# A scheduler that may let VectorE or GpSimd stand still for the port they share, with all its ranks set anew

## The chip, the cores and the metric

One core of a Trainium2 chip. The metric is the device time of one execution in microseconds (us), lower is better. The core has TensorE (matrix multiply, PE in the profile, its weight loads PEld), VectorE (DVE), ScalarE (ACT), GpSimd (POOL) and SyncE (SP), which here issues the DMAs. Each engine runs its own instructions strictly in the order in which the program gives them.

## The reference

```python
# q, k, v: (2, 8, 576, 64); three stages, all float32
scores = q @ k.T / sqrt(64)
kth = np.partition(scores, -32, axis=-1)[..., -32:-31]
attn = softmax(np.where(scores >= kth, scores, -1e9))
x = (attn @ v)                       # -> (1152 tokens, 512)
h = x @ moe_w_in;  x = (h * np.tanh(log1p(exp(h)))) @ moe_w_out    # 512 -> 2048 -> 512
h = x @ moe2_w_in; out = (h * sigmoid(h)) @ moe2_w_out             # 512 -> 2048 -> 512
```

The weights arrive as 64-bit floats and are turned into 32-bit floats on the chip.

## The kernel before

**Tiles.** The 1152 tokens are nine tiles of 128. Attention works on a tile and a pair of heads: 36 such pairs, four to a tile. A pair's way is: the q tile is split into a high and a low part (`qs`, line 279 or 277 for the high part, 285 or 287 for the low one), TensorE makes the scores (L373, `ps_att`), ScalarE or VectorE copies them to `sc`, VectorE finds the 32 largest of each row by four MAX8 (L389, `m`) and three MATCH_REPLACE8 (L392, `rest`) a head. Then, for tiles 0 to 5, ScalarE makes the exponentials `e` (L405) and VectorE masks and sums them (L409, which reads `sc` and `e`); for tiles 6 to 8 a mask is made by ScalarE (L415), subtracted on GpSimd or VectorE (`e` on L285 or L287) and ScalarE's exponential sums (L422). TensorE turns `e` (L434), the copies go to `pt`, TensorE multiplies by `v` (L450, L452, `ps_misc`), the row sums are inverted, spread and turned (L457 to L466), and VectorE multiplies (L475) into `xt`, the input of the first block. Line numbers of helpers stand for many uses: L277 is a copy on ScalarE, L279 one on VectorE, L285 a two-input operation on GpSimd, L287 the same on VectorE.

**Blocks.** The two feed-forward blocks take the tiles in groups: block 1 in [0], [1], [2], [3,4], [5,6], [7,8]; block 2 in [0,1], [2], [3,4], [5,6], [7,8]. Groups marked 'n' multiply in plain float32, groups marked 'r' with operands split into two parts and three passes. A group's first product is L625 (`ps_h`; L717 for the very first group), its second L696 (block 1) or L803 (block 2) into `ps_y`. Group [0,1] of block 2 needs block 1 of both tiles. 64 weight units are converted the first time they are used (L500 twice and L512 on ScalarE, L504 and L514 on GpSimd, the last giving `wraw`) and stored as float32 in DRAM; the 'r' groups split them again into `ws` (L277/L279, L285/L287), or read the splits back.

**Order.** `Plan` writes the whole program's order. `add` notes a step with the ways to do it (an engine, a cost, a flex added to the rank, and whether it takes the port that VectorE and GpSimd share: all of GpSimd's, and VectorE's fast copies and two-input operations from SBUF). A step's rank is its tile's or group's start plus a step (`TILES`, `DUE1`, `DUE2`), less the boost of its kind (`OFF`), plus the flex of its way (`FLEX`, or `FLEX1` for ranks below `EARLY`). `emit` then plays the program with its own costs: of all the steps that could go next it takes the one with the least key, a time first and the rank second. A step that can begin within `PEEK` of its engine's free time has that free time as its key, so steps of one engine are then sorted by rank. `port` is the time at which the shared port comes free. No step computes anything else for being placed elsewhere; only the order on each engine, the engine of steps with two ways, and the order of the DMA issues depend on these numbers.

Of the kernel before, what the change touches and what calls it, by code (L numbers as in the profile page):

```python
# [28 lines left out]
BLOCK1 = [([0], 'n'), ([1], 'n'), ([2], 'n'), ([3, 4], 'r'), ([5, 6], 'r'), ([7, 8], 'r')]  # L29
BLOCK2 = [([0, 1], 'n'), ([2], 'n'), ([3, 4], 'r'), ([5, 6], 'r'), ([7, 8], 'r')]  # L30

TILES = [(27.37, 9.86), (57.91, 10.94), (103.1, 10.19), (209.13, 7.03), (210.76, 10.65), (248.61, 48.9), (293.47,
         17.23), (429.14, 22.89), (434.19, 29.14)]
DUE1 = [(59.64, 30.74), (73.56, 12.7), (180.72, 34.18), (251.34, 30.85), (303.68, 119.16), (534.81, 11.0)]
DUE2 = [(192.15, 71.0), (274.42, 49.15), (480.58, 43.53), (598.12, 89.99), (800.13, 295.82)]

SBUF_BUFS = dict(kraw=1, kk=5, v=5, qraw=2, qs=2, sc=4, rest=1, e=1, pt=2, m8=10, bias=10, den=8, x=3, dt=2, xt=1,
                 wraw=9, ws=8, hs=2, th=1, wide=3, y=2, o=2)
PSUM_BUFS = dict(att=2, misc=1, h=3, y=2)

FLEX = dict(khi=-194.73, klo=-148.49, qhi=-16.01, qlo=-130.13, whi=-223.66, wlo=264.55, ghi=-13.66, glo=-274.69,
            hs=253.61, mk=197.2, se=96.17, den=6.96, y=300.0, sc=-176.69, pt=185.3, dt=-250.49, xlo=300.0)
FLEX1 = dict(khi=77.4, klo=230.65, qhi=-36.04, qlo=246.7, whi=-229.64, wlo=-300.0, ghi=-164.53, glo=194.85, hs=254.09,
             mk=120.49, se=None, den=-73.24, y=None, sc=300.0, pt=None, dt=267.41, xlo=-300.0)
EARLY = 566.61

OFF = dict(kload=416.67, qload=339.58, k=13.66, q=-14.61, sp=196.22, sc=127.3, bias=145.14, e=187.12, tp=155.23,
           pt=377.16, av=14.57, x=469.8, den=223.26, dw=224.3, dp=142.13, xt=253.71, m=0.66, cload=-5.6, cpn=-65.41,
           cse=12.49, cw=-42.16, cmid=46.37, wload=312.03, wsplit=-142.7, wstore=141.3, g=-146.58, hs=-58.75, y=394.7,
           th=516.12)  # L50

PEEK = 0.1
ADD = 1

HBM = 4
# [13 lines left out]
class Plan:  # L69
# [12 lines left out]
    def add(self, ways, reads=(), writes=(), uses=(), rank=0.0, boost=0.0, table=None, load=0.0):  # L82
# [3 lines left out]

        first = rank - (boost if not isinstance(boost, str) else OFF[boost])
        offset = lambda o: o if not isinstance(o, str) else FLEX1[o] if rank < EARLY and o in FLEX1 else FLEX[o]
        ways = [(w[0], w[1], offset(w[2]), w[3], w[4] if len(w) > 4 else w[0] == "pool") for w in ways
# [16 lines left out]
    def emit(self):  # L106
        steps = self.steps
        last, readers, users, turn = {}, {}, {}, {}
        for i, s in enumerate(steps):
            deps = set()  # L110
            for k in s["reads"]:
                deps |= last.get(k, set())
            for k in s["writes"]:
                deps |= last.get(k, set()) | readers.get(k, set())
            deps.discard(i)
            s["deps"], s["then"] = len(deps), []
            s["at"] = 0.0
            for d in deps:
                steps[d]["then"].append(i)
            for k in s["writes"]:  # L120
                last[k], readers[k] = {i}, set()
            for k in s["reads"]:
                readers.setdefault(k, set()).add(i)
            for k, t in s["uses"]:
                if k not in users:
                    turn.setdefault(t, []).append((s["rank"], len(users), k))
                users[k] = users.get(k, 0) + 1
        turn = {t: [k for _, _, k in sorted(v, reverse=True)] for t, v in turn.items()}
        free = {e: 0.0 for e in ("pe", "dve", "act", "pool", "sp")}
        dma, hw, port = 0.0, 0.4, 0.0  # L130
        table = None
        slots = {t: [0.0] * n for t, n in self.bufs.items()}
        held, ends, bank = set(), {}, {}
        queue, waiting = {e: set() for e in free}, {}
        for i, s in enumerate(steps):
            if not s["deps"]:
                for w in s["ways"]:
                    queue[w[0]].add(i)
        left = len(steps)
        while left:  # L140
            best = None
            stuck = []
            for e, q in queue.items():
                for i in q:
                    s = steps[i]
                    way = next(w for w in s["ways"] if w[0] == e)
                    at = max(s["at"], free[e], port if way[4] else 0.0)
                    took = {}
                    for k, t in s["uses"]:
                        if k not in held:  # L150
                            n = took[t] = took.get(t, 0) + 1
                            if len(slots[t]) < n or turn[t][-n] != k:
                                at = None
                                stuck.append((t, i))
                                break
                            at = max(at, slots[t][n - 1])
                        elif k in bank and bank[k][0] != e:
                            at = max(at, bank[k][1])
                    if at is None:
                        continue  # L160
                    rank = s["first"] + way[2]
                    key = (at, rank, i) if at > free[e] + PEEK else (free[e], rank, i)
                    if best is None or key < best[0]:
                        best = (key, e, i, at)
            if best is None:
                raise RuntimeError("no step can start")
            for t, i in stuck:
                for w in steps[i]["ways"]:
                    queue[w[0]].discard(i)
                waiting.setdefault(t, set()).add(i)  # L170
            _, e, i, at = best
            s = steps[i]
            moved = set()
            for w in s["ways"]:
                queue[w[0]].discard(i)
            _, cost, _, fn, shared = next(w for w in s["ways"] if w[0] == e)
            for k, t in s["uses"]:
                if k not in held:
                    held.add(k)
                    slots[t].pop(0)  # L180
                    turn[t].pop()
                    moved.add(t)
                    ends[k] = 0.0
            if s["table"] and s["table"] != table:
                cost += self.TABLE
                table = s["table"]
            at = max(at, free[e])
            if e == "pe":
                end = self.run_pe(at, cost)
            else:  # L190
                end = at + cost
            fn()
            free[e] = end
            if shared:
                port = end
            if e == "sp":
                hw = max(hw, at) + 0.55
                dma = max(dma, hw + 1.0) + s["load"] / 335e3
                end = max(end, dma + 1.4 - self.WAIT["sp"])
            for k, t in s["uses"]:  # L200
                if t.startswith("ps_"):
                    bank[k] = (e, end + self.WAIT[e])
                ends[k] = max(ends[k], end)
                users[k] -= 1
                if not users[k]:
                    slots[t].append(ends[k] + self.WAIT[e])
                    slots[t].sort()
                    moved.add(t)
            for t in moved:
                for j in waiting.pop(t, ()):  # L210
                    for w in steps[j]["ways"]:
                        queue[w[0]].add(j)
            for j in s["then"]:
                n = steps[j]
                n["at"] = max(n["at"], end + self.WAIT[e])
                n["deps"] -= 1
                if not n["deps"]:
                    for w in n["ways"]:
                        queue[w[0]].add(j)
            left -= 1  # L220
# [19 lines left out]
def kernel(ctx: ExitStack, tc, qh, kh, va, w1i, w1o, w2i, w2o, out):  # L240
# [580 lines left out]
    ystep = {}  # L821
    for t, (start, step) in enumerate(TILES):
        for p in range(NPAIR):
            attention(t, p, start + p * step)
    for g, (start, us) in enumerate(DUE1):
        block1(g, start, us)
    for g, (start, us) in enumerate(DUE2):
        block2(g, start, us)
# [48 lines left out]
```

## Time and profile before

| | |
|---|---|
| median of 3 runs | 670.81 us (668.43 to 670.87) |
| profiled execution | 671.01 us, span 669.2 us |
| busy | PE 606.7, PEld 534.9, DVE 533.7, ACT 468.0, POOL 392.2 us |
| moved by DMA | 178.32 MB |

The span is the time from the first to the last instruction in the profile; the profiled execution's own time is 1.8 us above it. A busy time is the sum of an engine's instructions, overlaps counted once. Groups of the profile list what ended the idle time before an instruction ("<-").

### The profile page before, as it was taken

To read this page: it belongs to the slowest core of one execution; us is meant where nothing else is said; L and a number is where in the kernel's file an instruction comes from. 1 tells how busy PE (TensorE), PEld (TensorE's weight loads), DVE (VectorE), ACT (ScalarE), POOL (GpSimd) and SP (SyncE) were. 2 spreads that over 40 slices of the span, in tenths; PEclk is the share of its full clock that TensorE was granted. 3 is DMA by queue.
4 is the path that set the end of the run, shared out by engine and by line. 5 is a ranking of instruction groups with operands and counts; after the bars stand their busy time and mean duration, and the time that the engine had idled before them with its cause. 6 is when DMAs were issued, how large, how long until landed. Compare 5 with 4: busy or idle time off the path is not lost.

```text
span 669.2 us, 13044 instructions
## 1 busy us (share of the span) xinstructions
PE 606.7 (91%) x4536; PEld 534.9 (80%) x4536; DVE 533.7 (80%) x1111; ACT 468.0 (70%) x973; POOL 392.2 (59%) x347
## 2 busy tenths in 40 slices
PE   1359857999999999989999999999999999999997
PEld 1248746998999966668799858999988799999996
DVE  4999998998999999799989898999989332434451
ACT  6779898699599999979985644977884543322321
POOL 6987648636477779886674212748973224554440
PEclk9999876999999999999999999999999999999999
DMA  9958538888899777899799797884669989876752
GB/s 311 314 175 256 193 120 282 281 289 302 272 299 323 243 227 274 272 349 317 266 369 409 226 325 238 279 272 155 219 228 305 369 289 320 285 244 236 268 174 82
DMA packets 85649, 178.32 MB, mean 266 GB/s; under 512 B 8144, under 2 KB 29136, under 8 KB 85584
## 3 DMA queue, kind: packets, MB, share of 16 engines
q1 hardware_dynamic: 85584, 177.50, 78.6%
q8 instruction: 35, 0.57, 0.3%
q14 instruction: 30, 0.25, 0.1%
HBM read 138.94 MB, written 38.54 MB: 265 GB/s over the span
## 4 chain that ended last, share of the span: by engine, by line
PE 46%; DVE 26%; ACT 15%; DMA 5%; issue 5%; POOL 2%; SPq 0%; DVEq 0%; ACTq 0%; POOLq 0%
PE ps_h L625 19%; DVE m L389 10%; PE ps_y L803 9%; PE ps_y L696 9%; DVE rest L392 8%; ACT ws L500 3%; PE ps_att L373 3%; PE ps_misc L450 3%; DVE e L409 2%; PE ps_att L434 2%; DMA wide<-in_w1i_dram 2%; DVE ws L287 2%; ACT wraw L512 2%; ACT pt L277 2%; ACT sc L277 1%
## 5 line engine op out<-in xcount | busy, mean ns | idle before, releaser
L389 DVE MAX8 m<-rest 128x8 f32<-128x576 f32 x216 | 155.4, 751 | 0.1
L285 POOL TENSOR_TENSOR ws<-wraw,ws 128x512 fp32r<-128x512 f32 x57 | 74.1, 1306 | 60.2 <-DVE ws L279 50.6
L504 POOL TENSOR_TENSOR ws<-ws 128x512 int32<-128x512 int32 x64 | 86.5, 1357 | 36.4 <-ACT ws L500 33.8
L392 DVE MATCH_REPLACE8 rest<-m,rest 128x576 f32<-128x576 f32 x144 | 106.8, 746 | 0.0
L500 ACT ACTIVATE ws<-wide,zone 128x512 int32<-128x512 int16 x128 | 94.8, 773 | 6.2 <-DMA wide<-in_w1o_dram 4.0
L373 PE MATMUL ps_att<-kk,qs 128*128 128x288 f32 x320 | 70.6, 341 | 26.9 <-POOL kk L285 17.1
L514 POOL TENSOR_TENSOR wraw<-wraw,ws 128x512 int32<-128x512 int32 x64 | 84.3, 1326 | 14.3 <-ACT wraw L512 10.7
L373 PEld LDWEIGHTS ps_att<-kk,qs 128*128 128x128 f32 x320 | 50.2, 202 | 35.5 <-POOL kk L285 24.8
L625 PEld LDWEIGHTS ps_h<-y,ws 128*128 128x128 f32 x576 | 73.3, 188 | 2.9
L625 PE MATMUL ps_h<-y,ws 128*128 128x256 f32 x576 | 75.6, 280 | 0.0
L625 PE MATMUL ps_h<-xt,ws 128*128 128x256 f32 x576 | 72.4, 282 | 0.1
L696 PE MATMUL ps_y<-wide,ws 128*128 128x256 f32 x540 | 71.2, 283 | 0.0
L625 PEld LDWEIGHTS ps_h<-xt,ws 128*128 128x128 f32 x576 | 69.3, 188 | 1.6 <-issue 1.0
L434 PE MATMUL ps_att<-ident,e 128*128 128x128 f32 x324 | 53.4, 289 | 17.7 <-DVE e L409 12.0
L696 PEld LDWEIGHTS ps_y<-wide,ws 128*128 128x128 f32 x540 | 66.2, 188 | 0.0
L803 PE MATMUL ps_y<-ws,wide 128*128 128x512 f32 x252 | 64.6, 396 | 0.0
L285 POOL TENSOR_TENSOR wide<-hs,wide 128x512 fp32r<-128x512 f32 x24 | 35.2, 1473 | 46.0 <-DVE wide L279 39.7
L434 PEld LDWEIGHTS ps_att<-ident,e 128*128 128x128 f32 x324 | 38.6, 147 | 28.4 <-DVE e L409 14.7
L696 PE MATMUL ps_y<-hs,wraw 128*128 128x128 f32 x384 | 52.3, 283 | 8.1 <-POOL wraw L514 4.5
L277 ACT COPY sc<-ps_att 128x288 f32<-128x288 f32 x120 | 44.9, 404 | 16.8 <-PE ps_att L373 16.2
L696 PEld LDWEIGHTS ps_y<-hs,wraw 128*128 128x128 f32 x384 | 48.6, 197 | 9.5 <-POOL wraw L514 5.4
L389 DVE MAX8 m<-sc 128x8 f32<-128x576 f32 x72 | 53.0, 751 | 2.1 <-ACT sc L277 1.8
(88 smaller groups left out, 1222.0 us busy)
## 6 DMA issues: line engine op xcount, KB each, us to landing
wraw<-w1i SPq DMA_DIRECT2D x64, 256.0 KB, 5.0
wraw<-w2i SPq DMA_DIRECT2D x64, 256.0 KB, 3.7
ws<-w1o_split SPq DMA_DIRECT2D x30, 512.0 KB, 4.8
ws<-w2o_split SPq DMA_DIRECT2D x28, 512.0 KB, 3.9
wraw<-w1o SPq DMA_DIRECT2D x48, 256.0 KB, 5.2
wide<-in_w1i_dram SPq DMA_DIRECT2D x16, 512.0 KB, 5.9
wide<-in_w1o_dram SPq DMA_DIRECT2D x16, 512.0 KB, 4.4
wide<-in_w2i_dram SPq DMA_DIRECT2D x16, 512.0 KB, 4.7
```

What stands on the lines that cost most here:

```text
L277: ways.append(("act", act_us(n, psum), act, lambda: nc.scalar.copy(get_out(), get_in())))
L285: ways.append(("pool", pool_us(n), pool, lambda: nc.gpsimd.tensor_tensor(out=get_out(), in0=get_a(), in1=get_b(), op=op)))
L373: nc.tensor.matmul(o, lhsT=l, rhs=r[:, f * SH:(f + 1) * SH], start=(i == 0), stop=(i == len(ops) - 1))
L389: add([("dve", 0.67, 0, lambda i=i, h=h, src=src: nc.vector.max(out=m8()[:, h, 8 * i:8 * i + 8], in_=src()[:, h]))], reads=srck, writes=[K ...
L392: add([("dve", 0.73, 0, lambda i=i, h=h, src=src: nc.vector.match_replace(out=rest()[:, h], in_to_replace=m8()[:, h, 8 * i:8 * i + 8], in_ ...
L434: nc.tensor.transpose(o[:, i, :], ef[:, (c + i) * P:(c + i + 1) * P], ident)
L500: add([("act", act_us(UNIT) + 0.14, 0, lambda i=i: nc.scalar.activation(pn()[:, i], top(), AF.Relu, scale=ONE16 - 2 * ONE16 * i, bias=zone))],
L504: ways = [("pool", pool_us(UNIT), 0, lambda: nc.gpsimd.tensor_tensor(out=se(), in0=pn()[:, 0], in1=pn()[:, 1], op=ALU.subtract))]
L514: add([("pool", pool_us(UNIT), 0, lambda: nc.gpsimd.tensor_tensor(out=w().bitcast(I32), in0=w().bitcast(I32), in1=se(), op=ALU.add))], rea ...
L625: nc.tensor.matmul(hp[:, c, :], lhsT=l, rhs=rr, start=(i == 0), stop=(i == len(ops) - 1))
L696: nc.tensor.matmul(yp[:, o, :], lhsT=l[:, d * P:(d + 1) * P], rhs=rr[:, c, :], start=(fc == 0 and k == 0 and o == 0), stop=last, skip_grou ...
L803: nc.tensor.matmul(op, lhsT=gg[:, c, i * P:(i + 1) * P], rhs=wt, start=(fc == 0 and k == 0), stop=(fc == NFC - 1 and k == len(ops) - 1))
```

## The change

The scheduler's loop used to put the port into a step's earliest time: a step that needs the port later than `PEEK` after its engine's free time was sorted by the time at which the port comes free, behind any step that can begin at once. Now the port is looked at apart: a step that waits for the port alone, and for at most `PORT` = 0.34 us, is still sorted by rank at its engine's free time, so the engine may stand still for it. `PEEK` falls from 0.1 to 0.05. All ranks, boosts and flexes have new values.

```diff
-TILES = [(27.37, 9.86), (57.91, 10.94), (103.1, 10.19), (209.13, 7.03), (210.76, 10.65), (248.61, 48.9), (293.47,
-         17.23), (429.14, 22.89), (434.19, 29.14)]
-DUE1 = [(59.64, 30.74), (73.56, 12.7), (180.72, 34.18), (251.34, 30.85), (303.68, 119.16), (534.81, 11.0)]
-DUE2 = [(192.15, 71.0), (274.42, 49.15), (480.58, 43.53), (598.12, 89.99), (800.13, 295.82)]
+TILES = [(19.37, 6.76), (46.36, 14.1), (106.73, 4.63), (204.37, 9.99), (225.06, 11.69), (258.55, 49.85), (345.98,
+         18.22), (519.3, 17.23), (461.45, 16.83)]
+DUE1 = [(55.53, 32.57), (72.6, 11.18), (185.18, 33.6), (264.74, 3.6), (326.98, 167.36), (749.26, 11.24)]
+DUE2 = [(194.98, 61.15), (262.2, 26.21), (504.62, 78.52), (783.18, 203.62), (946.46, 197.95)]
...
-FLEX = dict(khi=-194.73, klo=-148.49, qhi=-16.01, qlo=-130.13, whi=-223.66, wlo=264.55, ghi=-13.66, glo=-274.69,
-            hs=253.61, mk=197.2, se=96.17, den=6.96, y=300.0, sc=-176.69, pt=185.3, dt=-250.49, xlo=300.0)
-FLEX1 = dict(khi=77.4, klo=230.65, qhi=-36.04, qlo=246.7, whi=-229.64, wlo=-300.0, ghi=-164.53, glo=194.85, hs=254.09,
-             mk=120.49, se=None, den=-73.24, y=None, sc=300.0, pt=None, dt=267.41, xlo=-300.0)
-EARLY = 566.61
+FLEX = dict(khi=-199.43, klo=-179.86, qhi=-300.0, qlo=65.82, whi=259.95, wlo=-153.31, ghi=-62.92, glo=163.54,
+            hs=286.73, mk=-58.0, se=-300.0, den=105.07, y=271.68, sc=-47.47, pt=57.06, dt=-238.16, xlo=98.83)
+FLEX1 = dict(khi=245.84, klo=30.36, qhi=-26.57, qlo=179.72, whi=-172.94, wlo=-208.13, ghi=-191.1, glo=300.0, hs=19.48,
+             mk=8.23, se=None, den=-282.09, y=None, sc=252.9, pt=None, dt=239.76, xlo=-232.84)
+EARLY = 553.02
...
-OFF = dict(kload=416.67, qload=339.58, k=13.66, q=-14.61, sp=196.22, sc=127.3, bias=145.14, e=187.12, tp=155.23,
-           pt=377.16, av=14.57, x=469.8, den=223.26, dw=224.3, dp=142.13, xt=253.71, m=0.66, cload=-5.6, cpn=-65.41,
-           cse=12.49, cw=-42.16, cmid=46.37, wload=312.03, wsplit=-142.7, wstore=141.3, g=-146.58, hs=-58.75, y=394.7,
-           th=516.12)
-
-PEEK = 0.1
+OFF = dict(kload=578.07, qload=135.46, k=16.71, q=-13.88, sp=314.62, sc=197.87, bias=39.06, e=246.77, tp=342.92,
+           pt=330.03, av=-14.23, x=487.41, den=300.22, dw=35.2, dp=222.21, xt=191.17, m=-75.12, cload=96.71,
+           cpn=-97.42, cse=5.37, cw=-99.8, cmid=-37.21, wload=572.6, wsplit=-171.63, wstore=206.7, g=-82.77, hs=-40.2,
+           y=-31.25, th=709.1)
+
+PEEK = 0.05
+
+PORT = 0.34
...
-                    at = max(s["at"], free[e], port if way[4] else 0.0)
+                    at = max(s["at"], free[e])
...
-                    key = (at, rank, i) if at > free[e] + PEEK else (free[e], rank, i)
+                    soon = at <= free[e] + PEEK
+                    if way[4] and port > at:
+                        at, soon = port, soon and port <= free[e] + PORT
+                    key = (free[e] if soon else at, rank, i)
```

## Rows read from the trace of the kernel before

**Rows 1.** The page's head, busy times, slices and the chain by engine.
```profile
span 669.2 us, 13044 instructions
PE 606.7 (91%) x4536; PEld 534.9 (80%) x4536; DVE 533.7 (80%) x1111; ACT 468.0 (70%) x973; POOL 392.2 (59%) x347
...
PE   1359857999999999989999999999999999999997
...
DVE  4999998998999999799989898999989332434451
...
PE 46%; DVE 26%; ACT 15%; DMA 5%; issue 5%; POOL 2%; SPq 0%; DVEq 0%; ACTq 0%; POOLq 0%
```

**Rows 2.** Busy time by stretch: PE, PEld, DVE, ACT, POOL, then clock and DMA.
```profile
0.00:53.00 53.00, 19.66 (x97) 15.55 (x98) 41.93 (x88) 40.05 (x78) 43.03 (x44) 1.00 0.83 261
53.00:121.00 68.00, 54.23 (x398) 46.02 (x397) 63.91 (x142) 62.21 (x133) 43.43 (x37) 0.85 0.64 211
121.00:205.00 84.00, 83.06 (x704) 79.08 (x703) 80.28 (x177) 69.33 (x137) 46.95 (x49) 1.00 0.88 299
205.00:345.00 140.00, 134.33 (x969) 107.83 (x968) 135.43 (x284) 130.88 (x277) 110.10 (x97) 1.00 0.84 286
345.00:425.00 80.00, 77.02 (x602) 65.68 (x601) 70.32 (x153) 45.54 (x108) 27.61 (x28) 1.00 0.87 302
425.00:530.00 105.00, 102.94 (x816) 94.27 (x815) 92.56 (x195) 77.36 (x180) 67.26 (x55) 1.00 0.76 259
530.00:669.20 139.20, 135.47 (x963) 126.46 (x961) 49.27 (x78) 42.69 (x66) 53.87 (x41) 1.00 0.71 241
```

**Rows 3.** Groups of VectorE from 9 to 121 us: busy us, mean ns, idle before.
```profile
L389 DVE MAX8 m<-rest 128x8 f32<-128x576 f32 x50 | 36.0, 752 | 0.1
...
L409 DVE SCALAR_TENSOR_TENSOR e<-sc,m,e 128x576 f32<-128x576 f32 x16 | 16.2, 1044 | 0.5 <-ACT e L405 0.5
...
L279 DVE COPY sc<-ps_att 128x288 f32<-128x288 f32 x8 | 3.6, 456 | 9.2 <-PE ps_att L373 9.0
```

**Rows 4.** VectorE in order of time, 6 to 12, 39 to 50 and 112 to 122 us.
```profile
8.70 0.94 DVE L279 COPY sc<-ps_att 128x288 f32<-128x288 f32 x2 [8.70 <-PE ps_att L373]
...
40.53 1.97 DVE L409 SCALAR_TENSOR_TENSOR e<-sc,m,e 128x576 f32<-128x576 f32 x1
...
113.13 0.29 DVE L475 TENSOR_TENSOR xt<-ps_misc,dt 128x128 f32<-128x128 f32 x1 [1.56 <-PE ps_misc L452]
...
114.70 0.82 DVE L409 SCALAR_TENSOR_TENSOR e<-sc,m,e 128x576 f32<-128x576 f32 x1
...
120.40 0.28 DVE L475 TENSOR_TENSOR xt<-ps_misc,dt 128x128 f32<-128x128 f32 x1
```

**Rows 5.** GpSimd in order of time, 39 to 50 us.
```profile
39.95 1.93 POOL L285 TENSOR_TENSOR kk<-kraw,kk 64x576 fp32r<-64x576 f32 x1
```

**Rows 6.** Lines L409 and L287, the whole span: ns min/median/max, first and last start.
```profile
L409 DVE SCALAR_TENSOR_TENSOR e<-sc,m,e x48: 795/818/1967, 39.8 to 398.3; 128x576 f32<-128x576 f32 x48
...
L287 DVE TENSOR_TENSOR ws<-wraw,ws x52: 672/690/1791, 280.8 to 556.4; 128x512 fp32r<-128x512 f32 x52
```

**Rows 7.** Groups of the whole span, shapes apart.
```profile
L504 POOL TENSOR_TENSOR ws<-ws 128x512 int32<-128x512 int32 x64 | 86.5, 1357 | 36.4 <-ACT ws L500 33.8 <-DMA wraw<-w1o 1.0 <-DMA wraw<-w1i 0.8
L514 POOL TENSOR_TENSOR wraw<-wraw,ws 128x512 int32<-128x512 int32 x64 | 84.3, 1326 | 14.3 <-ACT wraw L512 10.7 <-issue 1.2 <-POOL qs L285 1.1
...
L409 DVE SCALAR_TENSOR_TENSOR e<-sc,m,e 128x576 f32<-128x576 f32 x48 | 44.5, 959 | 0.6 <-ACT e L405 0.5
...
L287 DVE TENSOR_TENSOR ws<-wraw,ws 128x512 fp32r<-128x512 f32 x52 | 43.2, 860 | 5.3 <-ACT ws L277 5.0
...
L625 PE MATMUL ps_h<-y,ws 128*128 128x256 f32 x576 | 75.6, 280 | 0.0
...
L803 PE MATMUL ps_y<-ws,wide 128*128 128x512 f32 x252 | 64.6, 396 | 0.0
...
L285 POOL TENSOR_TENSOR e<-sc,e 128x576 f32<-128x576 f32 x24 | 34.3, 1448 | 12.2 <-ACT e L415 12.2
```

**Rows 8.** Waits of TensorE: 53 to 121 us, then 205 to 345 us.
```profile
PE ps_y L696 <- POOL wraw L514: 4.5, 2, 2.6
PE ps_y L696 <- issue: 3.4, 1, 3.4
...
PE ps_h L625 <- POOL wraw L514: 2.7, 2, 1.4
PE ps_att L373 <- ACT sc L277: 1.3, 2, 1.1
```

**Rows 9.** Line L514, the whole span: first and last start.
```profile
L514 POOL TENSOR_TENSOR wraw<-wraw,ws x64: 1266/1280/1875, 12.2 to 323.7; 128x512 int32<-128x512 int32 x64
```

**Rows 10.** The chain that ended last, its end: start us, us, what.
```profile
530.47 18.37 PE ps_h L625 x156
...
655.66 9.82 PE ps_y L803 x42
```

**Rows 11.** VectorE in order of time, 515 to 531 us: the last attention pair.
```profile
529.18 0.29 DVE L475 TENSOR_TENSOR x<-ps_misc,dt 128x128 f32<-128x128 f32 x1 [2.24 <-PE ps_misc L452]
```

**Rows 12.** Groups from 205 to 345 us: conversions on GpSimd.
```profile
L514 POOL TENSOR_TENSOR wraw<-wraw,ws 128x512 int32<-128x512 int32 x28 | 37.5, 1348 | 4.5 <-ACT wraw L512 2.4 <-issue 1.2 <-POOL qs L285 0.2
```

## The prediction

> **What bounds the kernel now.** I read the page first: TensorE is busy for 606.7 of 669.2 us, its slices are thin only at the start, and the chain that ended last is 46% TensorE and 26% VectorE [rows 1]. So the question is where TensorE's other 62.5 us lie. The table of stretches answers it (stretch less busy time): 33.3 us from 0 to 53, 13.8 from 53 to 121, 0.9 to 205, 5.7 to 345, 3.0 to 425, 2.1 to 530, 3.7 to the end [rows 2]. Three quarters lie before 121 us. There VectorE is the bound: from its first instruction at 8.7 us it is busy for 41.9 + 63.9 = 105.8 of 112.3 us [rows 2, 4], mostly on the top-32 search [rows 3] of tiles 0 and 1. What ends the stretch can be named: the last product of tile 1 starts at 120.40 us [rows 4]; only then has TensorE the first block of tile 1 and, behind it, the second block of group [0,1].
>
> From 205 to 345 us nothing is slack: VectorE 135.4, ScalarE 130.9, TensorE 134.3 of 140 us [rows 2], with the rest of the weight conversions in it (the last L514 starts at 323.7 [rows 9]). From 530 us on TensorE runs without a break: 156 matmuls in 18.37 us, 118 ns each, at the end 42 in 9.82, 234 ns each [rows 10]. Nothing an order can do makes this stretch shorter, unless work leaves it for a hole further ahead.
>
> A busy matmul row hides its own slack: the weight loads are busy 79.1 of 84 us from 121 to 205, but 107.8 of 140 from 205 to 345 [rows 2]. Part of that is other matmul shapes, so I take the 5.7 us as a lower bound of what that stretch has to give.
>
> **How much VectorE may be delayed later.** The last pair's product is made at 529.2 us [rows 11]; 140 us of span follow. What must come after it is group [7,8] in both blocks: 576 L625 matmuls belong to three groups, 192 each, at 118 ns 22.6 us; block 1's second product is of the same count and shape; block 2's is (252 + 36 on kept weights) / 3 = 96 at 234 ns, 22.5 us [rows 7, 10]. Together some 90 us. So attention may end up to about 50 us later without setting the end, provided that TensorE has other groups to work on meanwhile. VectorE's own time counts up to 121 us and hardly behind it.
>
> **The change, part by part.** No arithmetic is added or removed; engines of steps with two ways, order, and DMA order move.
>
> *The port rule.* What it can act on is the time that port users lose. L409 takes 818 ns in the median and up to 1967 [rows 6]; the 1.97 us one at 40.53 us lies beside a GpSimd operation of 1.93 us from 39.95 to 41.88 [rows 4, 5]. Over the span, L409 loses 48 x (959 - 818) = 6.8 us and the low parts on L287 52 x (860 - 690) = 8.8 us [rows 6, 7]; up to 121 us, 16 x (1044 - 818) = 3.6 us [rows 3, 6]. The rule does not forbid these losses; it lets an urgent port user go ahead of a MAX8 when the port is at most 0.34 us away, and pays with an idle engine. Bounds up to 121 us: a gain of the 3.6 us at the most; a loss of 17 port users (16 L409 and a cast) x 0.34 = 5.8 us if each waits its full third. A MAX8 put in between holds VectorE for 0.75 us [rows 3], longer than the wait it fills, and behind an L409 stand the turn, the copy, the values and the product (114.70 to 120.40 for tile 1's last [rows 4]), so I take 1 us of gain. PEEK's halving goes with it at nothing: the work it shifts is at most 0.1 us apart.
>
> The trace's long stalls are around 1 us, not a third: 1.97 - 0.82 = 1.15 us for the one at 40.53 [rows 4, 6]. The Trainium skill (SBUF — State Buffer, Who interferes with whom) says why that is the natural size: whoever issues first holds the shared pair for its whole instruction and the other is blocked, whatever a plan meant. By that rule each stand-still that the plan sets at 0.34 us could become a whole GpSimd operation, 1.3 us; by the row the plan's wait and the chip's agree in most cases, since most L409 take the median. The trace bears the rule out at 40.53. I give it a rival of its own below.
>
> *Tiles and the first 121 us.* Tiles 0, 1 and 2 keep their order on VectorE: search ranks 19 to 40, 46 to 89, 107 to 121 now, against 27 to 57, 58 to 91, 103 to 134. MAX8 and MATCH_REPLACE8 have no boost, so the same pairs follow one another. What can move is the idle 112.3 - 105.8 = 6.5 us [rows 2] and the score copies on VectorE, 3.6 us [rows 3]. The scores' boost rises by 118, the score copies' by 71, the turns' by 188: the next pair's scores should be there sooner, and gaps like the 1.56 us before 113.13 us [rows 4], in which VectorE waited for TensorE, are those that this fills. Against it, VectorE's flex for score copies falls by 47, which can put more of them there. Bounds 0 to 6.5 us of gain; I take 3, the smaller half, since some gaps are latency of a single pair. With the port's 1 us, tile 1 is ready 4 us sooner and TensorE's full stretch begins 4 us sooner.
>
> *Conversions.* Boosts fall by 32 (cpn, ScalarE), 84 (cmid, ScalarE), 58 (cw, GpSimd) and 7 (cse), and the loads rise by 102. A unit is two L500 and one L512 on ScalarE, and L504 and L514, 1.36 + 1.33 us, on GpSimd [rows 7]. TensorE waited for L514 4.5 us up to 121 us and 2.7 us from 205 to 345 [rows 8]. Before 121 such a wait costs what it delays in attention behind it in TensorE's order, otherwise nothing, as TensorE lacks work anyway. Behind 205 it costs its whole length. GpSimd was busy 110 of 140 us there [rows 2], so conversions ranked later can still find room; ScalarE, at 131, has little. Bounds: +5.7 us of gain if all waits go; for the loss see the rivals.
>
> *Low parts, masks, copies.* The mask's flex falls from 120 to 8, so some of 24 L285 `e` go to VectorE. Each there costs about 690 x 576/512 = 780 ns (an estimate from L287 [rows 6]); all 24, 18.6 us, within the 50 us of allowance, and VectorE's idle time from 205 to 530 us (4.6 + 9.7 + 12.4 = 26.7 us [rows 2]) takes part of it: nothing on the end. The keys' low part, GpSimd's so far (1.93 us in [rows 5]), can now be VectorE's (its flex falls from 231 to 30); that shortens the way to the scores of a new pair and costs VectorE as much as one mask: nothing either. The `y` copies lose 426 of boost; there are groups enough to cover a late copy up to 530 us, and behind it the other open group covers it. DUE1[3] becomes a burst (30.9 to 3.6 us), and the last two block 2 groups now overlap (783 to 987, 946 to 1144), which gives TensorE a second stream where it is full already: nothing.
>
> *Sum.* 4 us up to 121, and 2.5 from 205 to 345 (just under half of 5.7, as the stretch is crowded on every engine), nothing elsewhere: 6.5. The span becomes 662.7; with the 1.8 us around it, 664.5 against 671.0 of the profiled execution, which stands 0.2 above the median of 670.8. Predicted: 664.5 us, its own range 655 to 667.5.
>
> **Rivals.** Half a per cent (667.5 to 674.2 us) is about what a measurement here can tell from no change.
>
> *Nothing moves.* The order of the searches stays, TensorE's full stretches stay full, and the 6.5 us of idle are latency. For it: the same first tiles; the full tail. Against it: 10 us of waits in the first 121 that a better order could cover. 667.5 to 674; chance 0.22.
>
> *Conversions come late (slower).* From 205 us on, L514 with its lower rank stands behind low parts on GpSimd and TensorE, in strict order, waits for `wraw`. 28 L514 fall in the stretch [rows 12]; each one late by one GpSimd operation costs 1.33 us [rows 7] on a full TensorE. Five of them cancel the gain of 6.5 (6.7 us); ten leave 671.0 - 6.5 + 13.3 = 677.8, fourteen 683. For it: 2.7 us of such waits already [rows 8], ScalarE at 94%. Against it: GpSimd's spare 30 us. 675 to 685; chance 0.21.
>
> *The stand-still becomes a full stall (slower).* 17 port users up to 121 us; if six more of them meet a whole GpSimd operation (1.15 us as at 40.53), that is 6.9 us on the stretch where VectorE sets the end, and with the other gains lost 671.0 + 6.9 = 677.9. It decides from about three on, 3.5 us. The page named above is the reason to expect it. Against it: half of the 48 L409 take 818 ns or less [rows 6], though GpSimd is busy for 86.5 of the first 121 us [rows 2]. Chance 0.07.
>
> *More than forecast.* All of 10.1 us up to 121 and all 5.7 us from 205 on: 655.2. From 121 to 205 the weight loads are busy for 0.94 of the time; at that share 140 us would hold 131.6, against 107.8 [rows 2], a gap of 24 us, most of it shape; a fifth of it would lead to 650. Chance 0.08.
>
> **How the numbers follow.** Forecast 0.42, more 0.08: faster 0.50. Nothing moves: same 0.22. The two slow cases: 0.28. The range leaves out about one in ten at either end: 650 to 680.
>
> **What would show it.** The last L475 of tile 1 at about 116 instead of 120.4 us; VectorE's idle from 9 to 121 us at 3 instead of 6.5; fewer L409 above 1 us before 121; TensorE idle from 205 to 345 at about 3 us and no longer wait for L514; the tail unchanged at 118 and 234 ns a matmul. The prediction is wrong if waits for `wraw` grow behind 205, if tile 1 is not ready sooner, or if TensorE starves between 345 and 530, where I expect nothing.

## The result and the profile after

654.23 us (median of 6 runs, 653.25 to 655.83) against 670.84 us (six runs of the kernel before): the ratio is 0.976 (95% interval 0.973 to 0.979), 16.6 us faster. I predicted faster by 6.5 us, 664.5 in a range of 650 to 680: the way was right and the time lies in the range, but the gain is two and a half times the forecast one. The profiled execution took 655.83 us with a span of 654.1, 15.1 less than before [rows 1].

Line numbers of the changed kernel are five higher: L409 is L414, L287 is L292, L475 is L480, L514 is L519. First the stretches (stretch, then busy PE, PEld, DVE, ACT, POOL, clock, DMA), as [rows 2]; the last one reaches past the end of this span:

```profile
0.00:53.00 53.00, 24.69 (x121) 19.41 (x121) 43.34 (x89) 42.52 (x84) 44.15 (x44) 1.00 0.89 282
53.00:121.00 68.00, 57.55 (x422) 50.33 (x423) 66.98 (x147) 66.58 (x146) 49.65 (x41) 0.87 0.71 232
121.00:205.00 84.00, 83.67 (x726) 79.58 (x725) 80.18 (x181) 72.46 (x145) 41.11 (x42) 1.00 0.87 293
205.00:345.00 140.00, 135.69 (x983) 110.16 (x981) 134.69 (x280) 124.48 (x261) 108.75 (x93) 1.00 0.89 307
345.00:425.00 80.00, 79.91 (x632) 69.69 (x633) 74.72 (x166) 57.06 (x134) 41.17 (x39) 1.00 0.84 290
425.00:530.00 105.00, 104.23 (x830) 96.37 (x827) 82.39 (x170) 74.18 (x166) 61.69 (x52) 1.00 0.78 267
530.00:669.20 139.20, 120.32 (x835) 111.42 (x833) 57.19 (x79) 39.05 (x63) 35.83 (x27) 1.00 0.62 207
```

TensorE's idle time, stretch less busy, against [rows 2]:

| us | 0 to 121 | 121 to 205 | 205 to 345 | 345 to 530 |
|---|---|---|---|---|
| before | 47.1 | 0.9 | 5.7 | 5.0 |
| after | 38.8 | 0.3 | 4.3 | 0.9 |
| predicted change | -4 | 0 | -2.5 | 0 |
| measured change | -8.3 | -0.6 | -1.4 | -4.2 |

That is 14.5 of the 15.1 us. From the last attention product on both kernels run the same full tail: it starts 140 us before the end in both (529.2 of 669.2 [rows 11], 513.9 of 654.1). The changed kernel's products (ns min/median/max, first and last start):

```profile
L480 DVE TENSOR_TENSOR x<-ps_misc,dt x24: 264/278/292, 200.5 to 513.9; 128x128 f32<-128x128 f32 x24
```

VectorE up to 121 us, by groups (busy us, mean ns, idle before), against [rows 3], then line L414 up to 121 us (ns min/median/max) and tile 1's last product (start us, us), against [rows 4]:

```profile
L394 DVE MAX8 m<-rest 128x8 f32<-128x576 f32 x54 | 38.6, 745 | 0.0
...
L414 DVE SCALAR_TENSOR_TENSOR e<-sc,m,e 128x576 f32<-128x576 f32 x16 | 17.8, 1136 | 0.0
...
L284 DVE COPY sc<-ps_att 128x288 f32<-128x288 f32 x5 | 2.3, 452 | 8.8 <-PE ps_att L378 8.7
```
```profile
L414 DVE SCALAR_TENSOR_TENSOR e<-sc,m,e x16: 800/938/1955, 22.0 to 108.7; 128x576 f32<-128x576 f32 x16
```
```profile
115.33 0.28 DVE L480 TENSOR_TENSOR xt<-ps_misc,dt 128x128 f32<-128x128 f32 x1
```

Tile 1 is ready at 115.33 instead of 120.40 us. VectorE is busy 43.34 + 66.98 = 110.3 us up to 121 instead of 105.8. It does not stall less at the port: the masking step's mean rose from 1044 [rows 3] to 1136 ns. What else moved stands in the order of the program: in the kernel before, up to 13 MAX8 of later pairs ran between a pair's last MAX8 and its masking on L409. Matching that order with the trace's times gives, for the pairs whose search ended before 121 us, a mean delay from the last MAX8 to the masking of 6.4 us (18.2 at the worst), and 1.6 in the changed kernel (6.4 at the worst). I call it the masking delay below. (It is slightly negative where one head is masked before the other's search ends.)

This delay is not all lost at the port. The masking also reads ScalarE's exponential, there is one buffer for `e`, and so a pair's exponentials wait until TensorE has turned the pair before. In the kernel before, the second pair's search ended at 32.3 us and its first exponential at 45.9, right before its masking. Counted from the later of the two inputs, for the head of a pair that is masked first, the mean wait is 4.2 us in the kernel before (19.7 at the worst, the very first pair) and 1.4 in the changed one (3.3 at the worst). The plan shows what that wait is: in the kernel before, the first pair's masking is ready at 20.1 us of the plan's own time and has a lower rank than every step that goes ahead of it, yet it is passed over 28 times in a row, up to 38.3 us. Each time the port comes free 0.2 to 1.2 us later than VectorE.

TensorE's wait for the masking up to 121 us (total, times, longest), before and after:

```profile
PE ps_att L434 <- DVE e L409: 10.3, 4, 7.6
```
```profile
PE ps_att L439 <- DVE e L414: 3.2, 2, 2.6
```

These 7.1 us are most of the 8.3 that TensorE's idle time fell by there.

### The profile page after: what moved, and what is told of

Same layout as the page of the kernel before. It is cut to its first block, busy times and chain, and to the rows that moved or that the text cites. A ratio compares the mean times of both kernels' runs of the same rounds, so it can differ in the third digit from the quotient of the medians.

```text
span 654.1 us, 13089 instructions
## 1 busy us (share of the span) xinstructions
PE 606.1 (93%) x4536; PEld 537.0 (82%) x4536; DVE 539.5 (82%) x1106; ACT 476.3 (73%) x993; POOL 382.3 (58%) x334
## 4 chain that ended last, share of the span: by engine, by line
PE 53%; DVE 16%; ACT 15%; DMA 7%; issue 4%; POOL 4%; SPq 1%; POOLq 0%; ACTq 0%
PE ps_h L630 20%; PE ps_y L701 12%; PE ps_y L808 11%; DVE m L394 6%; DVE rest L397 5%; ACT ws L505 4%; PE ps_att L378 3%; DMA wraw<-w1i 3%; PE ps_att L439 2%; PE ps_misc L455 2%; ACT wraw L517 2%; ACT pt L282 2%; ACT e L410 2%; DVE e L414 2%; POOL wraw L519 2%
## 5 line engine op out<-in xcount | busy, mean ns | idle before, releaser
L378 PE MATMUL ps_att<-kk,qs 128*128 128x288 f32 x320 | 72.8, 346 | 31.6 <-POOL kk L290 24.5
L282 ACT CAST ws<-wraw 128x512 fp32r<-128x512 f32 x93 | 57.4, 621 | 53.8 <-PE ps_h L630 25.3
L519 POOL TENSOR_TENSOR wraw<-wraw,ws 128x512 int32<-128x512 int32 x64 | 85.5, 1346 | 15.9 <-ACT wraw L517 11.0
L292 DVE TENSOR_TENSOR ws<-wraw,ws 128x512 fp32r<-128x512 f32 x65 | 58.9, 924 | 31.3 <-ACT ws L282 30.9
L290 POOL TENSOR_TENSOR ws<-wraw,ws 128x512 fp32r<-128x512 f32 x44 | 57.6, 1318 | 27.3 <-ACT ws L282 14.8
L290 POOL TENSOR_TENSOR wide<-th,wide 128x512 fp32r<-128x512 f32 x24 | 31.5, 1313 | 66.7 <-DVE wide L284 65.4
L290 POOL TENSOR_TENSOR wide<-hs,wide 128x512 fp32r<-128x512 f32 x24 | 32.0, 1342 | 49.4 <-DVE wide L284 40.2
```

What stands on the lines that cost most here:

```text
L282: ways.append(("act", act_us(n, psum), act, lambda: nc.scalar.copy(get_out(), get_in())))
L290: ways.append(("pool", pool_us(n), pool, lambda: nc.gpsimd.tensor_tensor(out=get_out(), in0=get_a(), in1=get_b(), op=op)))
L378: nc.tensor.matmul(o, lhsT=l, rhs=r[:, f * SH:(f + 1) * SH], start=(i == 0), stop=(i == len(ops) - 1))
L519: add([("pool", pool_us(UNIT), 0, lambda: nc.gpsimd.tensor_tensor(out=w().bitcast(I32), in0=w().bitcast(I32), in1=se(), op=ALU.add))], rea ...
```

## Experiments

**The rule and the numbers, each alone.** The loop of before is the new one with PORT = PEEK: a port user then counts as ready only if the port comes free within PEEK.

`rule_alone`: the new loop, and before's TILES, DUE1, DUE2, FLEX, FLEX1, EARLY, OFF and PEEK.

```diff
+PORT = 0.34
...
-                    at = max(s["at"], free[e], port if way[4] else 0.0)
+                    at = max(s["at"], free[e])
...
-                    key = (at, rank, i) if at > free[e] + PEEK else (free[e], rank, i)
+                    soon = at <= free[e] + PEEK
+                    if way[4] and port > at:
+                        at, soon = port, soon and port <= free[e] + PORT
+                    key = (free[e] if soon else at, rank, i)
```

> The new loop with PORT = 0.34, all numbers (PEEK too) those of before. Theory A (the numbers carry the gain, the rule by itself moves almost nothing): within 0.5% of before, 667.5 to 674 us. Theory B (the rule carries it, as urgent port users no longer stand behind a MAX8): at least half of the 16.6 us, 662 us or less. Theory C (the rule alone hurts, as the chip turns a planned third of a us into a whole GpSimd operation): 675 us or more, with more L409 above 1 us before 121 us.

Measured: 681.76 us, ratio 1.019 (1.016 to 1.022). The time is that of theory C, but its sign did not come: five masking steps above 1 us before 121, as in the kernel before, and a mean of 1014 ns. Up to 121 us this kernel is the better one (TensorE idle for 43.9 us instead of 47.1, masking delay 1.1); it loses behind, with 17.9 us idle up to 530 against 11.6. The profiled run, the fastest of six at 675.1, does not hold the last 6.7 us of the median; where those lie stays open. Its stretches (busy PE, PEld, DVE, ACT, POOL):

```profile
0.00:121.00 121.00, 77.07 (x541) 63.73 (x542) 110.02 (x240) 108.37 (x221) 91.69 (x84) 0.96 0.76 249
121.00:530.00 409.00, 391.14 (x3009) 341.05 (x3008) 376.69 (x792) 317.58 (x688) 243.84 (x219) 0.99 0.81 277
```

`ranks_alone`: before's loop with all of after's numbers.

> The loop of before with all numbers of after (PEEK 0.05). Theory A: 654 to 658 us. Theory B: 662 us or more. A third case, that the numbers were fitted to the rule and fall apart without it, would show as slower than before, above 674 us.

Measured: 670.89 us, ratio 1.002 (0.999 to 1.004).

Theories A and B both fall: neither part carries the gain. They only give it together. Where `ranks_alone` loses can be seen in one place (its line numbers are one higher than before's). The third pair's last MAX8 ended at 47.2 us and its exponentials, the first row here, at 51.2 and 51.9; its masking, the last row, begins at 66.34, 15.1 us after its last input. ScalarE's exponentials, then VectorE in order of time (start us, us), the end of that wait:

```profile
50.42 1.47 ACT L406 ACTIVATE e<-sc,bias 128x576 f32<-128x576 f32 x2
```
```profile
58.08 0.74 DVE L393 MATCH_REPLACE8 rest<-m,sc 128x576 f32<-128x576 f32 x1
...
59.46 1.41 DVE L390 MAX8 m<-rest 128x8 f32<-128x576 f32 x2
...
62.24 1.41 DVE L390 MAX8 m<-rest 128x8 f32<-128x576 f32 x2
...
65.01 1.41 DVE L390 MAX8 m<-rest 128x8 f32<-128x576 f32 x2
66.34 0.97 DVE L410 SCALAR_TENSOR_TENSOR e<-sc,m,e 128x576 f32<-128x576 f32 x1
```

GpSimd in the same time, and TensorE:

```profile
56.22 1.28 POOL L505 TENSOR_TENSOR ws<-ws 128x512 int32<-128x512 int32 x1 [0.26 <-ACT ws L501]
57.46 1.28 POOL L515 TENSOR_TENSOR wraw<-wraw,ws 128x512 int32<-128x512 int32 x1
58.69 2.51 POOL L505 TENSOR_TENSOR ws<-ws 128x512 int32<-128x512 int32 x2
61.15 2.51 POOL L515 TENSOR_TENSOR wraw<-wraw,ws 128x512 int32<-128x512 int32 x2
```
```profile
67.47 1.09 PE L435 MATMUL ps_att<-ident,e 128*128 128x128 f32 x4 [10.02 <-DVE e L410]
```

GpSimd runs one conversion behind the other. In the plan, whenever VectorE comes free the port is not (it comes free 0.07 to 1.24 us later, in all 22 turns that this masking loses), the masking step's key is the port's time, and a MAX8 that can begin at once goes first. When that MAX8 ends, GpSimd's next operation holds the port. So the masking of a finished pair waits not for one operation but for much of the search of the next pairs, 12 MAX8 here, and TensorE, with that pair's turn next in its strict order, stands for 10.02 us.

**One half of the numbers each.** `early_new` and `late_new` take the numbers by rank, below and from 150, both with the new loop.

```diff
-        first = rank - (boost if not isinstance(boost, str) else OFF[boost])
+        first = rank - (boost if not isinstance(boost, str) else (OFF_LO if rank < CUT else OFF_HI)[boost])
```

> The new loop; numbers of after for all ranks below 150 (tiles 0 to 2, block 1 of tiles 0 and 1), of before from there on. If the gain up to 121 us is the early numbers' own, some 6 to 8 us of it come: 662 to 665 us, with tile 1's last product at about 115 instead of 120.4 us. If the gain needs both parts, it stays within 0.5% of before.

Measured: 674.31 us, ratio 1.007 (1.004 to 1.009). The early stretch does as expected, TensorE's idle time up to 121 us is 40.0 us; behind it 16.6 us are idle up to 530, against 11.6 before. The expected total is missed, though tile 1's last product came at 112.8 us, sooner than the expected 115.

> The new loop; numbers of before for all ranks below 150, of after from there on. If the stretches add up, it gets the other part: tile 1's last product at about 120 us as before, TensorE's idle time from 205 to 530 us down from 10.7 to about 5 us, 660 to 664 us. If the late gain only follows from the earlier start, it stays within 0.5% of before.

Measured: 672.63 us, ratio 1.003 (1.001 to 1.006), 44.9 us idle up to 121 and 13.1 from there to 530. Missed too: the parts do not add up. (Boosts differ between the two sets, so steps on either side of the cut also change their order with each other.)

**Which port user it is.** The rule for VectorE's masking step alone, and for all the others.

```diff
-                        at, soon = port, soon and port <= free[e] + PORT
+                        at, soon = port, soon and port <= free[e] + (PORT if e == "dve" and s["kind"] == "e" and way[1] == 0.73 else PEEK)
```

> The changed kernel, but only VectorE's masking step of tiles 0 to 5 (the SCALAR_TENSOR_TENSOR on e) may wait a third of a us for the port; every other port user is treated as before (waits up to 0.05 us). Theory D (what the rule cures is that this step, which unlocks the turn, the values and the product of its pair, stood behind whole searches of later pairs, since GpSimd held the port whenever VectorE came free): the mean delay from a pair's last MAX8 to its masking stays near 1.3 us (old loop: 4.5 to 5) and the time stays within 1% of the changed kernel, 648 to 661 us. Theory S (the order of the changed kernel is a lucky one out of many, and any other order of the same rule falls back): 662 us or more although the delay stays short.

Measured: 660.25 us, ratio 0.986 (0.983 to 0.989); the mean masking delay over all 24 pairs is 1.6 us. That is theory D's range, at its upper end. Against `ranks_alone`, where no step may wait longer than 0.05 us, this one permission is worth 10.6 us.

> The complement: every port user but that masking step may wait a third of a us. Theory D: the mean delay rises to 4 us or more and the time to 664 to 674 us, most of the loss before 121 us. If the other port users carry the gain, 650 to 660 us.

Measured: 686.03 us, ratio 1.027 (1.022 to 1.032); mean delay 4.5 us. TensorE's stretches up to 121 us, first `after_e_only`, then `after_not_e` (busy PE, PEld, DVE, ACT, POOL):

```profile
0.00:121.00 121.00, 80.40 (x559) 67.67 (x560) 111.55 (x240) 110.79 (x234) 95.67 (x85) 0.97 0.79 258
```
```profile
0.00:121.00 121.00, 71.97 (x473) 61.12 (x474) 105.38 (x225) 102.25 (x201) 93.94 (x84) 0.90 0.79 255
```

One step decides between them: 8.4 us of TensorE up to 121. `after_not_e` is 12 us worse than expected, since more is lost behind 121 as well: 17.2 us idle up to 530, against 9.1.

`before_e_only`: the same edit on the numbers of before (PEEK 0.1).

> The numbers of before, and only the masking step may wait a third of a us (all else up to 0.1, as before). Theory D: tile 1's last product at about 115 us instead of 120.4, and TensorE's idle time up to 121 us at 40 to 43 us instead of 47; in time 660 to 667 us if nothing behind 121 us gets worse, while all port users together with these numbers took 1.9% more. Theory S: any time from 660 to 685 us, with no tie to the delay.

Measured: 667.81 us, ratio 0.996 (0.995 to 0.998); idle up to 121 us 43.0 instead of 47.1, and 13.3 instead of 11.6 from 121 to 530. The expected gain up to 121 is there, with tile 1's last product at 117.7 us rather than 115, and part of it is given back behind; the time misses its range by 0.8 us.

**Neighbours of one order.** Small changes of a number that leave the rule as it is.

```diff
-PORT = 0.34
+PORT = 0.30
```

> The changed kernel with PORT = 0.30 instead of 0.34: the same rule and the same numbers, another order. Theory D: 649 to 661 us. Theory S: 662 us or more, with the delay as short as in the changed kernel; the difference is then what one order out of its neighbours is worth.

Measured: 678.28 us, ratio 1.013 (1.007 to 1.019), with a mean delay of 1.0 us: theory S. Against the changed kernel it loses on both sides of 121 us: 48.3 us idle instead of 38.8, and 13.9 instead of 5.5 from there to 530. Up to 121 TensorE waits 6.5 us for the masking and 5.7 for `wraw` (3.2 and none in the changed kernel). A single place behind shows how such an order loses. VectorE, GpSimd and TensorE from 337 to 353 us:

```profile
337.00 2.97 DVE L284 CAST ws<-wraw 128x512 fp32r<-128x512 f32 x2
339.90 3.47 DVE L292 TENSOR_TENSOR ws<-wraw,ws 128x512 fp32r<-128x512 f32 x2
```
```profile
335.40 4.29 POOL L290 TENSOR_TENSOR wide<-hs,wide 128x512 fp32r<-128x512 f32 x3 [0.37 <-DVE wide L284]
339.65 3.17 POOL L290 TENSOR_TENSOR ws<-wraw,ws 128x512 fp32r<-128x512 f32 x2
```
```profile
352.90 1.34 PE L455 MATMUL ps_misc<-pt,v 128*64 128x128 f32 x10 [4.97 <-DVE x L480]
```

Two casts and two low parts of VectorE took 6.4 us beside GpSimd operations with no gap between them; the two low parts alone 3.47, where two take 1.38 at the median of before [rows 6]. TensorE's next products then stood 4.97 us for VectorE's product of the pair before, which was late by about as much (that the one led to the other is argued from their order). The Trainium skill (SBUF — State Buffer, Who interferes with whom) says of VectorE's two-port mode that whoever issues first gets the shared pair for the whole instruction and the other engine is blocked, and that a VectorE instruction with two SBUF inputs contends with GpSimd's reads too; these rows agree.

> The changed kernel with tile 0's start at 19.87 instead of 19.37, nothing else. Theory S (the time is mostly that of one order out of many): 660 to 680 us. Theory D alone (the rule decides, any order with it is about as good): 650 to 659 us. The delay from search to masking should be short in either.

```diff
-TILES = [(19.37, 6.76),
+TILES = [(19.87, 6.76),
```

Measured: 665.01 us, ratio 0.995 (0.992 to 0.998): theory S.

> The changed kernel with the first second-block group's start at 195.48 instead of 194.98, nothing else. The first 100 us should stay nearly as they are. Theory S: up to 121 us as in the changed kernel, 660 to 675 us in all. Theory D alone: 650 to 659 us.

```diff
-DUE2 = [(194.98, 61.15),
+DUE2 = [(195.48, 61.15),
```

Measured: 664.42 us, ratio 0.991 (0.988 to 0.994); 39.3 us idle up to 121 as in the changed kernel, 13.3 from there to 530 against its 5.5: theory S again.

> The kernel before with PEEK at 0.12 instead of 0.1: the old rule, another order. Theory S holds for the old kernel too, which was one chosen order: 675 to 690 us. Theory D alone: 667 to 675 us. The mean delay stays at 4 us or more in either.

Measured: 685.67 us, ratio 1.024 (1.020 to 1.028). The order of before was a chosen one too.

> The changed kernel, in which the masking step alone may wait up to 1.30 us for the port, a whole GpSimd operation; all other port users keep 0.34. If the delay that is left (6 us at two pairs before 50 us) were worth something, the mean delay falls below 1 us and the time to 646 to 653 us. Theory S: another order again, 660 to 680 us, whatever the delay.

```diff
-                        at, soon = port, soon and port <= free[e] + PORT
+                        at, soon = port, soon and port <= free[e] + (1.30 if e == "dve" and s["kind"] == "e" and way[1] == 0.73 else PORT)
```

Measured: 670.86 us, ratio 1.002 (1.000 to 1.005). The delay falls to -0.8 us, and the time does not follow: theory S. TensorE's waits from 53 to 121 us (total, times, longest), first here, then in the changed kernel:

```profile
PE ps_att L439 <- DVE e L414: 12.0, 7, 2.8
```
```profile
PE ps_att L439 <- DVE e L414: 3.2, 2, 2.6
```

The masking steps themselves now stand at the port (median 1161 ns up to 121 us, against 938), and the turns behind them hold up TensorE; its idle time up to 121 us is 48.8. In this order, the only one tried, waiting for a whole operation costs what it was to save; part of the 16.6 us may be the order's, as with the other neighbours.

**The rule, off and on, at nudged numbers.** Three partners, so that the rule alone makes the difference.

> The changed kernel with tile 0's start at 19.87 and PORT = PEEK = 0.05, which is the loop of before: the partner of the first nudge (665.0 us). If the rule itself is worth its shorter delay, this is slower than its partner, 671 to 686 us, TensorE idle for 47 us or more up to 121 us and VectorE for 15 or more. If the rule is worth nothing on average and the changed kernel only a lucky order, 658 to 670 us.

Measured: 671.88 us, ratio 1.002 (1.000 to 1.005), as the case in which the rule is worth its shorter delay has it.

> The changed kernel with the first second-block group at 195.48 and PORT = PEEK = 0.05: the partner of the second nudge (664.4 us). The same two cases: 671 to 686 us with 47 us or more of idle TensorE up to 121 us, or 658 to 670 us.

Measured: 676.07 us, ratio 1.011 (1.007 to 1.014), the same case.

> The numbers of before with PEEK = 0.12 and only the masking step allowed to wait 0.34 us: the partner of the run with PEEK = 0.12 (685.7 us). If the rule is worth its shorter delay, 670 to 681 us, TensorE's idle time up to 121 us falling from 51.5 to 45 us or less. If not, 680 to 692 us.

Measured: 683.75 us, ratio 1.022 (1.018 to 1.026). In time it falls where the rule is worth nothing, 1.9 us from its partner and within the two intervals; in TensorE's idle time up to 121 us, 42.8, it does as the rule's case has it.

The pairs, with `rule_alone` against before as the sixth (idle is stretch less busy, from the table of stretches; VectorE's holds the 8.7 us before its first instruction; PE's wait is that for the masking up to 121 us; the delay is that of the pairs before 121 us). "On" is the full rule for the first three and the last, and the masking step alone for the fourth and fifth:

| numbers | us off, on | PE idle to 121 | PE's wait | DVE idle to 121 | PE idle 121 to 530 | masking delay |
|---|---|---|---|---|---|---|
| after | 670.9, 654.2 | 48.1, 38.8 | 11.6, 3.2 | 18.9, 10.7 | 9.3, 5.5 | 7.9, 1.6 |
| after, tile 0 at 19.87 | 671.9, 665.0 | 47.5, 42.6 | 11.4, 5.2 | 17.4, 10.2 | 12.6, 10.5 | 5.7, 2.8 |
| after, group at 195.48 | 676.1, 664.4 | 50.0, 39.3 | 11.8, 4.0 | 18.3, 9.4 | 14.9, 13.3 | 7.9, 1.6 |
| before | 670.8, 667.8 | 47.1, 43.0 | 10.3, 3.6 | 15.2, 12.4 | 11.6, 13.3 | 6.4, 1.0 |
| before, PEEK 0.12 | 685.7, 683.8 | 51.5, 42.8 | 11.0, 4.6 | 15.5, 10.2 | 19.5, 18.7 | 8.2, 1.0 |
| before, full rule | 670.8, 681.8 | 47.1, 43.9 | 10.3, 3.6 | 15.2, 11.0 | 11.6, 17.9 | 6.4, 1.1 |

Up to 121 us the two sides do not overlap. All nine kernels in which the masking may wait 0.34 us have TensorE idle for 38.8 to 44.9 us there, the six in which it may not for 47.1 to 51.5. But the two with another limit, 0.30 and 1.30 us, stand at 48.3 and 48.8, short delay or not.

## Why the prediction was right or wrong

**The step that failed is "The port rule", taken at 1 us.** I priced it by the time that port users lose inside their own rows, 3.6 us up to 121, and by one MAX8 put in between. What the rule removes is not in those rows: the masking step lost its turn again and again while GpSimd held the port, and stood behind up to 13 MAX8. It could have been read from the start of the first L409 at 39.8 us [rows 6], though the search of the first pair had ended at 21.6 us, and from TensorE's wait for the masking, 10.3 us up to 121. In the six pairs the rule takes 3.2 to 10.7 us, 6.8 on average and 9.3 at the new numbers, off TensorE's idle time up to 121 us, where I had 1 us for it and 4 in all. With `after_e_only` against `after_not_e` it is the masking step alone that differs, and 8.4 us. A limit of 0.30 or 1.30 us did not bring this gain, so it belongs to a good order with the rule, not to any order with it. PEEK, which I put at nothing, is no such small term either: 0.02 more of it cost the kernel before 14.9 us.

**"Nothing elsewhere" was wrong as well.** From 345 to 530 us TensorE's idle time fell from 5.0 to 0.9 us. The new numbers have this with the old loop too (1.0 in `ranks_alone`), and the two nudges keep it (1.0 and 1.2) while they lose from 205 to 345 us (9.3 and 11.8 against 4.3); other neighbours lose it (6.4 with PORT = 0.30). The changed kernel's 5.5 us from 121 to 530 are the least of all 17 kernels with a profile; the other 16 lie between 9.1 and 19.5, with either rule and either set of numbers. Half a unit on one rank costs 5.0 or 7.8 us of it. In time the first five pairs gain 1.9 to 16.7 us with the rule, 8.0 on average, and the sixth loses 11. So about half of the gain lies up to 121 us, where the wait for the masking goes away, and the rest is one good order among many; what the rule is worth in time on its own is not shown. That the order was good was measured; why this one, rather than its neighbours, has fewer waits there stays open. I counted a reordering as the sum of its pieces, and `early_new` and `late_new` show that the pieces do not add.

**The parts that held.** Tile 1's last product came at 115.3 us (expected about 116), and VectorE's idle time from its start to 121 us fell to 2.0 us (expected 3), but not for my reason: I had 3 of the 4 us from the new numbers of "Tiles and the first 121 us", and with the old loop these bring none, the product at 126.6 us and VectorE idle for 10.2 (`ranks_alone`). That these two figures came out was luck; it is the rule, by which the masking may wait for the port, that brings them. The tail stayed full. The waits for `wraw` from 205 to 345 us fell from 2.7 us [rows 8] to 0.5; the idle time there fell by 1.4 instead of 2.5. "Tiles and the first 121 us" said that the same pairs follow one another, which holds for the start of the searches only.

**The rivals.** "Conversions come late" did not happen: the last L519 starts at 296.6 us, 27 sooner than before [rows 9], though its boost fell. The line in the changed kernel (ns min/median/max, first and last start):

```profile
L519 POOL TENSOR_TENSOR wraw<-wraw,ws x64: 1263/1284/1853, 12.4 to 296.6; 128x512 int32<-128x512 int32 x64
```

"The stand-still becomes a full stall" happened in part. I expected fewer masking steps above 1 us before 121; there are 7 instead of 5, and their loss is 16 x (1136 - 814) = 5.2 us, 814 being the median over the span, instead of 3.6. It is outweighed by searches that are no longer in the way. "More than forecast" came nearest: 655.2 us. "Nothing moves" rested on searches that keep their order, and fell with it.

## What to carry to other kernels

In a list scheduler, look for a ready step that loses its turn repeatedly: take the time from the end of its last input (all of them, not only the nearest) to its start, not the length of its own row, and look for the engine that stands waiting for it. A step that needs a resource which another engine holds back to back may find it taken at its own engine's free time again and again, 28 times here, and must be allowed a short wait; 0.34 us was enough here, while 0.30 and 1.30 us, each in the one order tried, were not better than none. When an order comes out of many ranks, time a few neighbours of it before crediting a change: here they lay 1.6 to 3.7% above the chosen order, as much as the change itself is worth.

## What the runs showed of the hardware that I had not expected

The faster plan had more stalls at the port: the low parts on L292 lose 65 x (924 - 693) = 15.0 us, on L287 before 8.8 us. It got faster all the same, as 12.3 of the 15.0 us lie behind 530 us, where VectorE is busy for less than half of the time. (There are 13 more low parts on VectorE; whether the rule or the new numbers put the stalls there is not shown.) The changed kernel's group on L292 (busy us, mean ns, idle before), then its line (ns min/median/max):

```profile
L292 DVE TENSOR_TENSOR ws<-wraw,ws 128x512 fp32r<-128x512 f32 x65 | 58.9, 924 | 31.3 <-ACT ws L282 30.9
```
```profile
L292 DVE TENSOR_TENSOR ws<-wraw,ws x65: 666/693/1824, 294.8 to 632.8; 128x512 fp32r<-128x512 f32 x65
```
